# Reads of single words of k, q and w_in on ScalarE's queue in a gated-attention and MLP kernel

## The chip, the cores and the metric

One core of one Trainium2 chip runs the whole program. The metric is device time in microseconds (us), taken as the median of several runs. The engines are TensorE (PE; its weight loads are listed apart as PEld), VectorE (DVE), ScalarE (ACT), GpSimd (POOL) and SyncE (SP). In this kernel SP does no arithmetic; it issues DMAs.

## The reference

A gated linear attention over 4 batches, 8 heads, 768 tokens and head size 48 is followed by a two-layer MLP on 3072 tokens of width 384, with hidden width 2048. All data are float32.

```python
f = 1.0 / (1.0 + np.exp(-f_logit))                 # q, k, v, f_logit: (4, 8, 768, 48)
for t in range(S):
    state = f[:, :, t, :, None] * state + np.einsum('bhd,bhe->bhde', k[:, :, t], v[:, :, t])
    y[:, :, t] = np.einsum('bhd,bhde->bhe', q[:, :, t], state)
x = np.ascontiguousarray(y.transpose(0, 2, 1, 3)).reshape(B * S, H * D)     # (3072, 384)
h = x @ w_in                                       # w_in: (384, 2048)
g = np.maximum(0.01 * h, h)
out = g @ w_out                                    # w_out: (2048, 384)
```

## The kernel before

**Units.** The recurrence is worked in chunks of 128 tokens. The work is cut into 12 units. Units 0 to 3 are "paired": unit j takes the first two chunks (256 tokens, `2 * C`) of batch j, with two neighbouring tokens on each of 128 partitions, and its loads come in two halves of four heads each. Units 4 to 11 take one later chunk of two batches each.

**A unit's way.** `load` brings f, k, q and v from DRAM into the tiles `raw_fk` (f and k) and `raw_qv` (q and v). On ACT, `gate_e` and `gate_l` turn f into the log of the gate; PE sums it up over the chunk (`cs`); ACT makes decays of it (`dec`: the tiles `em`, `at` and `end`). `scale` multiplies k and q by decays, on DVE or POOL (tiles `kh` and `qh`); PE turns them (`tk`, `tq`), multiplies them to scores (`sc`), which DVE masks (`mk`), and mixes them with v (`mx`). `x_out` copies the result as `xT`. The MLP's first layer is `up` or `up_pair` (lines 510 and 521), ACT's leaky relu follows, `down` (line 532) is the second layer, `out_copy` and `store` bring the result out. `fill` puts matmuls of a constant tile on PE (line 135) that nothing reads.

**Weights.** `load_w_in` and `load_w_in_half` bring 512 or 256 columns of w_in, with row 128 k + p on partition p, into spare raw tiles; `cast_w` and `cast_w_in_half` make bfloat16 tiles of them on ACT, DVE or POOL. w_out follows in the same way.

**Order.** Nothing schedules the work: a long string, `order`, is read word by word, and each word calls a part of the kernel with its numbers (`Lk_0_1` loads the second half of unit 0's k; `dec_1_1` is the second decay of unit 1; `WI_2` loads the third 512 columns of w_in, the first weights that are loaded). So each engine's instructions stand in the string's order. All DMAs of the kernel are issued by SP's queue.

**Semaphores.** The framework under the kernel hands the DMAs eight semaphores in turn, named DMAHW0 to DMAHW7. Before a semaphore is used again, the issuing queue waits until the DMA that had it has landed; a reader of loaded data waits for the semaphore of its load.

Of the kernel before, what the change touches and what calls it, by code (L numbers as in the profile page):

```python
# [9 lines left out]
FP32 = mybir.dt.float32  # L10
# [5 lines left out]
def kernel(  # L16
# [10 lines left out]
    nc = tc.nc  # L27

    B, H, S, D = q.shape
    assert (B, H, S, D) == (4, 8, 768, 48)  # L30
    C = 128
# [3 lines left out]
    NK, NF = KD // 128, FF // 128  # L35
# [16 lines left out]
    const = ctx.enter_context(tc.tile_pool(name="const", bufs=1))  # L52
    psum = ctx.enter_context(tc.tile_pool(name="psum", bufs=1, space=bass.MemoryType.PSUM))
    ctx.enter_context(tc.manual_schedule())

    nc.scalar.preload_act_table_set("natural_log_exp_and_others")

    def tiles(n, shape, dtype, name):
        return [const.tile(shape, dtype, name=f"{name}{i}", tag=f"{name}{i}") for i in range(n)]
# [47 lines left out]
    def on(e):  # L107
        return nc.gpsimd if e else nc.vector
# [30 lines left out]
    w_in_b = tiles(NW, [128, NK, 512], BF16, "w_in")  # L139
    w_out_b = tiles(NW, [128, 4, KD], BF16, "w_out")  # L140

    def staging(i):
        t = (raw_fk, raw_qv)[i % 2][NB - 2 + i // 2]
        return t.rearrange("t x a h d -> t (x a h d)")
# [14 lines left out]
    def load(x):  # L159
        def go(j, a, e=0):  # L160
            queue = nc.scalar if e else nc.sync
            if paired(j):
                h = slice(0, H) if a == 2 else slice(4 * a, 4 * a + 4)
                queue.dma_start(out=by_pair(raw(j, x))[:, h].rearrange("t h s d -> t h (s d)"),  # L164
                                  in_=srcs[x][j, h, 0:2 * C, :].rearrange("h (t s) d -> t h (s d)", s=2))
            else:
                c, h = units[j]
                queue.dma_start(out=raw(j, x)[:, a],  # L168
                                  in_=srcs[x][2 * h + a, :, c * C:(c + 1) * C, :].rearrange("h t d -> t h d"))
        return go  # L170

    def load_w_in(i):
        nc.sync.dma_start(out=staging(i).rearrange("t (k n) -> t k n", k=NK),
                          in_=moe_w_in[:, 512 * i:512 * i + 512].rearrange("(k p) n -> p k n", p=128))

    def half_of(t, x):
        return t[:, :, 256 * x:256 * x + 256]
# [17 lines left out]
    def cast_w(to):  # L195
        def go(i, x, e):
            cols = slice(512 * x, 512 * x + 512)
            dst, src = to[i].rearrange("t k n -> t (k n)")[:, cols], staging(i)[:, cols]
            if e == 1:
                nc.scalar.copy(out=dst, in_=src)  # L200
            else:
                on(e).tensor_copy(out=dst, in_=src)
        return go
# [361 lines left out]
    def store(j, a):  # L565
# [7 lines left out]
        "sc": score, "mk": mask, "mx": mix, "ms": mix_state, "xt": x_out, "pt": state, "sf": state_add, "sb": state_end,  # L573
        "up": up, "pr": relu, "uw": up_pair, "pw": relu_pair, "dn": down, "ob": out_copy, "st": store,
        "Lf": load("f"), "Lk": load("k"), "Lq": load("q"), "Lv": load("v"),
        "We": load_w_in_half, "Ce": cast_w_in_half, "WI": load_w_in, "WO": load_w_out, "CI": cast_w(w_in_b), "CO": cast_w(w_out_b),
        "dh": down_half, "oh": out_half, "sh": store_half,
        "c0": constants, "zk": clear_pads, "pm": make_pair_mask, "zv": clear_v2, "zs": clear_state, "ut": make_ut,
        "F": fill,
# [5 lines left out]
    Lv_1_0 gl_1_0 Lv_0_1 dec_0_0 Lq_1_1 ck_0_1_0 Lk_1_0 zv_2_1 zs_0_1 pm_1 tq_0_1@3 Lf_2_0 Lv_1_1 v_0_0 v_0_1 v_1_0  # L585
    cs_1_0@4 Lq_1_0 Lf_2_1 ge_1_1 WI_2 cq_0_1_0 gl_1_1 We_0_0 sc_0_1@5.6 k_0_0_0 F_3@0 tk_0_0@7 q_0_0_0 We_1_1
    dec_1_0 Lq_2_1 k_1_0_1 mk_0_1_0 ck_0_0_1 tq_0_0@0 cs_1_1@2 cq_0_0_0 v_1_1 F_1@4 sc_0_0@1.3 F_4@0 pt_0_2@4.5
    mk_0_1_1 dec_1_1 k_1_1_0 tk_1_1@0 q_1_0_1 q_1_1_0 mk_0_0_0 mk_0_0_1 sf_0_0 F_8@6 tq_1_1@7 sb_0_0 mx_0_2@6.2
    ge_2_0 CI_2_1_2 cq_1_1_0 Ce_0_0_0_2 ck_1_1_0 Ce_0_0_1_2 Lk_2_0 tk_1_0@1 sc_1_1@3.4 pt_1_2@7.0 Lk_2_1 xt_0_0_1
    F_1@6 tq_1_0@6 gl_2_0 ge_2_1 ms_0 Lq_2_0 ck_1_0_1 We_1_0 mk_1_1_0 gl_2_1 sf_1_0 We_0_1 Lv_2_0 cs_2_1@3 cs_2_0@1  # L590
    cq_1_0_1 sb_1_0 Lv_2_1 xt_0_1_0 sc_1_0@7.6 WI_3 CI_2_0_1 Ce_1_1_0_2 Ce_1_1_1_2 CI_2_2_0 mk_1_1_1 F_1@2 up_0_4@2
# [89 lines left out]
```

## Time and profile before

| | |
|---|---|
| median of 3 runs | 176.87 us (176.82 to 177.32) |
| profiled execution | 177.9 us, its span 175.9 us |
| busy: PE, PEld, DVE, ACT, POOL | 167.3, 105.0, 83.5, 107.5, 64.8 us |
| granted PE clock | 0.999 of full speed |
| DRAM read, written | 25.17 MB, 4.72 MB |
| DMA packets on SP's queue | 110512, 34.61 MB |

The span runs from the first to the last instruction of the profiled execution; the profiled execution's own time is 2.0 us longer than its span. Busy times are sums over the span and overlap between engines. A line number (L164) is the kernel's line; `out<-in` names tiles; "SPq" is SP's queue, and for a DMA issue the time shown is that of the issue, not of the transfer. In brackets stands the idle time of the engine just before an instruction and what ended it. A row "DMA to landing" gives the time from the start of an issue until all of its data are there.

### The profile page before, as it was taken

The page shows a single profiled execution, that of the slowest core. Times are in us where ns is not written, and L with a number is a line of the kernel's source. Part 1 is how long each engine was busy: PE and PEld are TensorE (multiplying, and loading weights), DVE is VectorE, ACT ScalarE, POOL GpSimd, SP SyncE. Part 2 cuts the span into 40 slices and gives each one's busy share as a digit, 9 for nine tenths or more (in the row PEclk, how much of TensorE's full clock was granted, in tenths as well). Part 3 has the DMA queues.
Part 4 walks back from the last instruction along what each step waited for, and adds up shares of the span by engine and source line. Part 5 has one row for each costly group of instructions (what it writes and reads, how often), then busy time and mean ns, then how long its engine had stood idle before and what let it go on. Part 6 is the DMA issues. An engine that isn't in the chain of part 4 may idle for free.

```text
span 175.9 us, 5142 instructions
## 1 busy us (share of the span) xinstructions
PE 167.3 (95%) x2095; PEld 105.0 (60%) x2095; DVE 83.5 (47%) x169; ACT 107.5 (61%) x233; POOL 64.8 (37%) x149
## 2 busy tenths in 40 slices
PE   7788989999999999999999999999999999999993
PEld 2555678797666785744565754565734555645662
DVE  4488787555138407602465770838622308510010
ACT  4775497797753681499960489900599930477411
POOL 7558686353401972200266565001462222000000
PEclk9999999999999999999999999999999999999999
DMA  5999999999999889897999999999989994132004
GB/s 125 279 296 312 317 292 364 364 306 247 241 198 198 149 175 197 159 200 150 197 240 139 248 217 218 177 147 188 267 174 213 173 200 126 46 137 93 0 22 157
DMA packets 110535, 34.93 MB, mean 199 GB/s; under 512 B 102960, under 2 KB 109744, under 8 KB 110512
## 3 DMA queue, kind: packets, MB, share of 16 engines
q1 hardware_dynamic: 110512, 34.61, 85.2%
q8 instruction: 16, 0.26, 0.6%
q14 instruction: 7, 0.06, 0.1%
HBM read 25.17 MB, written 4.72 MB: 170 GB/s over the span
## 4 chain that ended last, share of the span: by engine, by line
PE 63%; DMA 13%; SPq 11%; issue 4%; POOL 3%; DVE 3%; ACT 1%; POOLq 0%; DVEq 0%
PE ps L532 24%; PE ps L521 19%; PE ps L510 9%; SPq L164 6%; DMA out_dram<-osb 6%; SPq L168 5%; DMA raw_fk<-in_moe_w_in_dram 4%; PE ps L393 3%; DMA kT<-kh 3%; PE ps L548 2%; PE ps L362 1%; DVE wm L376 1%; POOL kh L286 1%; PE ps L258 1%; PE ps L463 1%
## 5 line engine op out<-in xcount | busy, mean ns | idle before, releaser
L532 PE MATMUL ps<-w_out,gT 128*128 128x384 bf16 x368 | 65.8, 326 | 0.0
L532 PEld LDWEIGHTS <-gT 128*128 128x128 bf16 x368 | 34.3, 98 | 22.5
L521 PE MATMUL ps<-xT,w_in 128*128 128x512 bf16 x192 | 44.4, 379 | 0.5 <-DVE osb L543 0.5
L525 ACT ACTIVATE gT<-ps 128x512 bf16<-128x512 f32 x64 | 35.1, 631 | 6.1 <-PE ps L521 6.0
L521 PEld LDWEIGHTS <-w_in 128*128 128x128 bf16 x192 | 18.4, 98 | 21.4 <-issue 1.3
L376 DVE TENSOR_TENSOR wm<-ps,ut 128x512 bf16<-128x512 f32 x32 | 19.9, 683 | 15.8 <-PE ps L362 6.2
L291 POOL CAST vb<-raw_qv 128x384 bf16<-128x384 f32 (+1 forms) x16 | 10.6, 664 | 37.0 <-DMA raw_qv<-in_v_dram 36.8
L510 PE MATMUL ps<-xT,w_in 128*128 128x256 bf16 x192 | 23.3, 273 | 0.8 <-ACT xT L445 0.5
L543 DVE COPY osb<-ps 128x384 f32<-128x384 f32 x14 | 7.6, 554 | 31.9 <-PE ps L532 19.2
L516 ACT ACTIVATE gT<-ps 128x512 bf16<-128x512 f32 x32 | 17.6, 624 | 5.7 <-PE ps L510 5.5
L510 PEld LDWEIGHTS <-w_in 128*128 128x128 bf16 x192 | 18.2, 98 | 3.9 <-ACT w_in L200 0.5
L229 ACT ACTIVATE e<-raw_fk 128x384 f32<-128x384 f32 (+1 forms) x16 | 10.9, 689 | 15.1 <-DMA raw_fk<-in_f_logit_dram 14.9
L274 ACT ACTIVATE em<-ps 128x384 bf16<-128x384 f32 x24 | 12.2, 508 | 11.5 <-PE ps L261 10.0
L445 ACT CAST xT<-ps 128x384 bf16<-128x384 f32 x14 | 6.7, 502 | 16.8 <-PE ps L393 16.6
L483 POOL CAST sb<-sf 64x192 bf16<-64x192 f32 x40 | 13.7, 343 | 8.2 <-DVE sf L473 6.0
L480 POOL TENSOR_TENSOR sf<-sf,end 128x192 f32<-128x192 f32 x16 | 8.1, 505 | 19.0 <-DVE sf L475 18.6
L286 DVE TENSOR_TENSOR kh<-raw_fk,em 128x384 bf16<-128x384 f32 (+1 forms) x10 | 8.7, 866 | 13.5 <-DMA raw_fk<-in_k_dram 7.1
L475 DVE TENSOR_TENSOR sf<-sf,ps 64x192 f32<-64x192 f32 x32 | 11.2, 350 | 5.1 <-PE ps L463 2.2
L286 DVE TENSOR_TENSOR qh<-raw_qv,at 128x384 bf16<-128x384 f32 (+1 forms) x12 | 9.3, 789 | 8.3 <-ACT at L275 7.8
L275 ACT ACTIVATE at<-ps 128x384 bf16<-128x384 f32 x24 | 12.4, 515 | 0.0
L286 POOL TENSOR_TENSOR kh<-raw_fk,em 128x384 bf16<-128x384 f32 (+1 forms) x6 | 8.5, 1410 | 8.1 <-ACT em L274 3.6
L241 ACT ACTIVATE lf<-e 128x384 bf16<-128x384 f32 (+1 forms) x16 | 10.9, 684 | 0.3
(92 smaller groups left out, 182.5 us busy)
## 6 DMA issues: line engine op xcount, KB each, us to landing
out_dram<-osb SPq DMA_DIRECT2D x23, 192.0 KB, 3.2
raw_fk<-in_f_logit_dram SPq DMA_DIRECT2D x22, 192.0 KB, 4.0
raw_fk<-in_k_dram SPq DMA_DIRECT2D x22, 192.0 KB, 4.0
raw_qv<-in_q_dram SPq DMA_DIRECT2D x22, 192.0 KB, 4.0
raw_qv<-in_v_dram SPq DMA_DIRECT2D x22, 192.0 KB, 4.0
raw_fk<-in_moe_w_out_dram SPq DMA_DIRECT2D x2, 768.0 KB, 8.4
raw_qv<-in_moe_w_out_dram SPq DMA_DIRECT2D x2, 768.0 KB, 7.3
raw_fk<-in_moe_w_in_dram SPq DMA_DIRECT2D x1, 768.0 KB, 6.7
```

Source lines behind the costliest of these rows:

```text
L229: nc.scalar.activation(e[:, part], src[:, part], AF.Exp, scale=-1.0)
L274: nc.scalar.activation(ems[j % 2][:, a], t[:, 0:H * D], AF.Exp, scale=1.0)
L275: nc.scalar.activation(ats[j % 2][:, a], t[:, 0:H * D], AF.Exp, scale=-1.0)
L286: eng.tensor_mul(heads(j, to[j % NR], a)[:, :, :, 0:D], raw_heads(j, x, a), decays(j, by, a))
L376: nc.vector.tensor_mul(w, src.rearrange("t (p n) -> t p n", p=P2), ut[:, None, :].to_broadcast([128, P2, 128]))
L475: nc.vector.tensor_add(sf[rows], sf[rows], new)
L483: nc.gpsimd.tensor_copy(out=sb[rows, :, y * D:y * D + D], in_=sf[rows])
L510: nc.tensor.matmul(pm[:, i, :], w_in_of(ff, kk), xTs[j // 2 % 2][:, kk, j % 2].rearrange("t a s -> t (a s)"), start=(kk == 0), stop=(kk == ...
L516: nc.scalar.activation(dst, pm, AF.Prelu, alpha=0.01)
L521: nc.tensor.matmul(banks[bank], w_in_of(ff, kk), xTs[j // 2 % 2][:, kk].rearrange("t u a s -> t (u a s)"), start=(kk == 0), stop=(kk == NK ...
L525: nc.scalar.activation(g_blocks(j)[ff], banks[st[j].pop(("pm", ff))], AF.Prelu, alpha=0.01)
L532: nc.tensor.matmul(po, g_of(j, ff, a), w_out_b[quarter][:, ff % 4, :], start=(ff == 0), stop=(ff == NF - 1))
```

## The change

Three DMAs are added, all issued by ACT. None of the loads changes, and nothing reads the words.

- Two stand ahead of everything else on ACT, also ahead of its table load. They read batch 0 of k and of q: from each of 8 heads, the first element of every sixteenth of the first 256 tokens, 128 words of 4 bytes each, into 16 partitions of a small tile.
- One, `tw`, stands in `order` after `dec_1_1`. It reads element 1024 of every eighth row of w_in, 48 words, into 16 partitions. Column 1024 is the first of those that `WI_2` loads.

```diff
     ctx.enter_context(tc.manual_schedule())
+
+    first_words = const.tile([16, 2, H], FP32, tag="first_words")
+    for i, t in enumerate((k, q)):
+        nc.scalar.dma_start(out=first_words[:, i], in_=t[0, :, 0:2 * C:16, 0].rearrange("h t -> t h"))
 
     nc.scalar.preload_act_table_set("natural_log_exp_and_others")
...
+    row_words = const.tile([16, NK], FP32, tag="row_words")
+
+    def touch_w_in():
+        nc.scalar.dma_start(out=row_words, in_=moe_w_in[::8, 1024].rearrange("(k p) -> p k", p=16))
...
+        "We": load_w_in_half, "Ce": cast_w_in_half, "WI": load_w_in, "tw": touch_w_in, ...
...
-    mk_0_1_1 dec_1_1 k_1_1_0 tk_1_1@0 q_1_0_1 ...
+    mk_0_1_1 dec_1_1 tw k_1_1_0 tk_1_1@0 q_1_0_1 ...
```

The lines of the changed kernel lie 4 to 9 further down (`load` issues at L168 there, not L164), and tile numbers after an underscore move by 3. What moves on the engines is shown in rows of the two programs' orders. First ACT, from its first row on: `e` is written by `gate_e` from unit 0's f, `lf` by `gate_l`. Before:

```order
L676 UNCONDITIONAL_BRANCH
L56 ACT_TABLE_LOAD
L229 ACTIVATE e_76<-raw_fk_64 128x384
L241 ACTIVATE lf_78<-e_76 128x4x2x48
L229 ACTIVATE e_76<-raw_fk_64 128x384
```

And of the changed kernel, the same place on ACT:

```order
L685 UNCONDITIONAL_BRANCH
L58 DMA first_words<-in_k_dram 16x8x1
L58 DMA first_words<-in_q_dram 16x8x1
L60 ACT_TABLE_LOAD
L238 ACTIVATE e_79<-raw_fk_67 128x384
L250 ACTIVATE lf_81<-e_79 128x4x2x48
```

The two issues stand ahead of the table load and of the first gate; the rest of the row follows as before. The third one stands on ACT between the last decay of unit 1 (`em`, `at`, `end`) and the first gate of unit 2:

```order
L283 ACTIVATE em_91<-ps_160 128x384
L284 ACTIVATE at_93<-ps_160 128x384
L286 ACTIVATE end_95<-ps_160 128x2x2
L183 DMA row_words<-in_moe_w_in_dram 16x3x1
L238 ACTIVATE e_79<-raw_fk_69 128x384
```

Nothing else is inserted there. On SP the loads stand as before, but the new DMAs take three semaphores out of the turn, so that SP's waits are for other DMAs. These are SP's sixth to tenth DMAs with their waits (the halves of k and f of units 0 and 1, then q and v), before:

```order
L164 DMA raw_fk_64<-in_k_dram 128x4x96
L164 DMA raw_fk_65<-in_f_logit_dram 128x4x96
L164 DMA raw_fk_65<-in_k_dram 128x4x96
L164 DMA raw_qv_70<-in_q_dram 128x4x96 [waits DMAHW0_49]
L164 DMA raw_qv_70<-in_v_dram 128x4x96 [waits DMAHW1_49]
```

and in the changed kernel:

```order
L168 DMA raw_fk_67<-in_k_dram 128x4x96
L168 DMA raw_fk_68<-in_f_logit_dram 128x4x96 [waits DMAHW0_49]
L168 DMA raw_fk_68<-in_k_dram 128x4x96 [waits DMAHW1_49]
L168 DMA raw_qv_73<-in_q_dram 128x4x96 [waits DMAHW2_49]
L168 DMA raw_qv_73<-in_v_dram 128x4x96 [waits DMAHW3_49]
```

Semaphores 0 and 2 belong to the words of k and q here, 1 and 3 to the two halves of unit 0's f. So SP's first wait comes two DMAs earlier, at its seventh. Farther on, at the loads around the first weights, with their waits in the changed kernel:

```order
L168 DMA raw_qv_74<-in_q_dram 128x4x96 [waits DMAHW3_49]
L168 DMA raw_fk_69<-in_f_logit_dram 128x4x96 [waits DMAHW4_49]
L177 DMA raw_fk_72<-in_moe_w_in_dram 128x3x512 [waits DMAHW5_49]
L189 DMA raw_fk_71<-in_moe_w_in_dram 128x3x256 [waits DMAHW6_49]
L189 DMA raw_qv_77<-in_moe_w_in_dram 128x3x256 [waits DMAHW7_49]
L168 DMA raw_qv_75<-in_q_dram 128x4x96 [waits DMAHW0_49]
```

Semaphore 7 belongs to the words of w_in there: SP's twentieth DMA, the half of w_in into `raw_qv`, waits for them. From SP's thirteenth DMA to its nineteenth the wait is for the DMA seven places earlier in SP's queue, where it was eight before. On PE, DVE and POOL the instructions stand as they did.

More of the change, by code (lines that the diff above doesn't have):

```diff
@@ L575 @@
         "Lf": load("f"), "Lk": load("k"), "Lq": load("q"), "Lv": load("v"),
-        "We": load_w_in_half, "Ce": cast_w_in_half, "WI": load_w_in, "WO": load_w_out, "CI": cast_w(w_in_b), "CO": cast_w(w_out_b),
+        "We": load_w_in_half, "Ce": cast_w_in_half, "WI": load_w_in, "tw": touch_w_in, "WO": load_w_out, "CI": cast_w(w_in_b), "CO": cast_w(w_out_b),
         "dh": down_half, "oh": out_half, "sh": store_half,
@@ L587 @@
     dec_1_0 Lq_2_1 k_1_0_1 mk_0_1_0 ck_0_0_1 tq_0_0@0 cs_1_1@2 cq_0_0_0 v_1_1 F_1@4 sc_0_0@1.3 F_4@0 pt_0_2@4.5
-    mk_0_1_1 dec_1_1 k_1_1_0 tk_1_1@0 q_1_0_1 q_1_1_0 mk_0_0_0 mk_0_0_1 sf_0_0 F_8@6 tq_1_1@7 sb_0_0 mx_0_2@6.2
+    mk_0_1_1 dec_1_1 tw k_1_1_0 tk_1_1@0 q_1_0_1 q_1_1_0 mk_0_0_0 mk_0_0_1 sf_0_0 F_8@6 tq_1_1@7 sb_0_0 mx_0_2@6.2
     ge_2_0 CI_2_1_2 cq_1_1_0 Ce_0_0_0_2 ck_1_1_0 Ce_0_0_1_2 Lk_2_0 tk_1_0@1 sc_1_1@3.4 pt_1_2@7.0 Lk_2_1 xt_0_0_1
```

## The prediction

> **What bounds the kernel now.** I read the page first, for engine shares.
>
> ```profile
> span 175.9 us, 5142 instructions
> PE 167.3 (95%) x2095; PEld 105.0 (60%) x2095; DVE 83.5 (47%) x169; ACT 107.5 (61%) x233; POOL 64.8 (37%) x149
> q1 hardware_dynamic: 110512, 34.61, 85.2%
> ```
>
> TensorE (PE) is busy 95% of a span of 175.9 us; nothing else passes 61%. A change that adds no PE work can only pay where PE waits, so I next cut the span into stages, by what DMA delivers. Columns: stage, its length, busy time (and instructions) of PE, PEld, DVE, ACT, POOL, then granted clock, DMA share, GB/s.
>
> ```profile
> 0.00:2.50 2.50, 1.45 (x4) 0.58 (x5) 1.67 (x11) 1.28 (x1) 1.76 (x12) 1.00 0.17 38
> 2.50:3.50 1.00, 1.00 (x4) 0.30 (x2) 0.32 (x3) 0.00 (x0) 0.85 (x7) 1.00 1.08 296
> 3.50:5.50 2.00, 2.00 (x13) 0.98 (x12) 0.00 (x0) 1.93 (x5) 2.00 (x8) 1.00 0.93 208
> 5.50:8.00 2.50, 1.62 (x19) 1.10 (x18) 1.69 (x4) 1.65 (x6) 1.37 (x6) 1.00 1.13 304
> 8.00:14.50 6.50, 5.56 (x104) 3.65 (x108) 5.56 (x11) 4.74 (x14) 3.62 (x10) 1.00 1.10 293
> 14.50:16.00 1.50, 1.20 (x76) 0.92 (x79) 1.24 (x4) 0.67 (x2) 1.25 (x4) 1.00 0.87 273
> 16.00:19.30 3.30, 2.66 (x77) 1.92 (x70) 1.92 (x5) 2.21 (x6) 1.54 (x3) 1.00 1.05 359
> 24.00:80.00 56.00, 55.93 (x772) 39.86 (x772) 28.20 (x57) 38.71 (x84) 23.65 (x45) 1.00 0.98 233
> 80.00:172.00 92.00, 90.99 (x949) 52.12 (x948) 38.70 (x70) 53.24 (x116) 24.50 (x50) 1.00 0.78 162
> ```
>
> From 24 us PE is full: 55.93 of 56.00 us, then 90.99 of 92.00. There is no room there, and none of the change's instructions stand there. Before 24 us the DMA share is near or above 1 in every stage after 2.5 us, so the input stream sets the pace, and in one stage it delivers badly: 208 GB/s from 3.5 to 5.5 us, between stages of 296 and 304. At 296 GB/s the same bytes need 2.0 × 208 / 296 = 1.41 us, so **0.6 us** is missing. A second, weaker dip is 273 GB/s at 14.5 to 16.0.
>
> Third, the first loads one by one (start of the issue, in us, and time from issue to landing).
>
> ```profile
> L164 SPq DMA_DIRECT2D raw_fk<-in_f_logit_dram x2: 449/468/488, 0.7 to 1.2; - x2
> DMA to landing us min/median/max: 2.8/2.8/2.8
> L164 SPq DMA_DIRECT2D raw_fk<-in_k_dram x1: 499/499/499, 1.8 to 1.8; - x1
> DMA to landing us min/median/max: 4.2/4.2/4.2
> L164 SPq DMA_DIRECT2D raw_qv<-in_q_dram x1: 507/507/507, 2.3 to 2.3; - x1
> DMA to landing us min/median/max: 4.3/4.3/4.3
> L164 SPq DMA_DIRECT2D raw_fk<-in_f_logit_dram x1: 508/508/508, 2.9 to 2.9; - x1
> DMA to landing us min/median/max: 4.3/4.3/4.3
> L164 SPq DMA_DIRECT2D raw_fk<-in_k_dram x1: 507/507/507, 3.4 to 3.4; - x1
> DMA to landing us min/median/max: 4.4/4.4/4.4
> ```
>
> The two loads of f land at 0.7 + 2.8 = 3.5 and 1.2 + 2.8 = 4.0. The first of k lands at 1.8 + 4.2 = 6.0, 2.0 us behind. The next three, q, f of unit one and the second half of k, land at 6.6, 7.2 and 7.8: 0.6 apart. So the first load of k, and with it all behind it, is 2.0 − 0.6 = **1.4 us** late on the DMA engine that finishes last, 0.6 us on the mean of 16 (the dip). The second load of k has other rows of the same tensor and shows no gap. So the wait reads like one for the first access to a tensor, which is what the change aims at; that is my reading, no view names the cause.
>
> Fourth, what the late landings hold up.
>
> ```profile
> 0.73 1.28 ACT L56 ACT_TABLE_LOAD   x1 [0.73 <-PEq L665]
> 3.51 0.52 ACT L229 ACTIVATE e<-raw_fk 128x384 f32<-128x384 f32 x1 [1.50 <-DMA raw_fk<-in_f_logit_dram]
> 6.07 0.56 DVE L286 TENSOR_TENSOR kh<-raw_fk,em 128x384 bf16<-128x384 f32 x1 [3.25 <-DMA raw_fk<-in_k_dram]
> 7.24 0.52 ACT L229 ACTIVATE e<-raw_fk 128x384 f32<-128x384 f32 x1 [0.82 <-DMA raw_fk<-in_f_logit_dram]
> 12.52 6.74 DMA raw_fk<-in_moe_w_in_dram
> 16.48 0.91 POOL L286 TENSOR_TENSOR qh<-raw_qv,at 128x384 bf16<-128x384 f32 x1 [0.72 <-DMA raw_qv<-in_q_dram]
> 17.45 0.40 PE L319 MATMUL ps<-ident,qh 128*128 128x128 bf16 x4 [0.51 <-POOL qh L286]
> 19.37 0.28 PE L135 MATMUL ps<-filler 128*128 128x256 bf16 x1
> 19.95 2.31 PE L510 MATMUL ps<-xT,w_in 128*128 128x256 bf16 x18 [0.30 <-ACT w_in L200]
> ```
>
> ScalarE (ACT) waits 0.82 us for unit one's f at 7.24. The load of w_in at 12.52 is a link of 6.74 us in the chain that ended last, and PE's first matmul from w_in at 19.95, from which PE runs nearly full, waits 0.30 for its cast. Just ahead, a scaled q that its load held up to 16.48 (0.72) holds PE until 17.45 (0.51). All of these are landings of one stream: shift the stream by x and PE's full stretch starts about x earlier, up to some 0.8 (ACT's 0.82). Beyond, compute binds.
>
> **The change part by part.** *Issues of the first words.* Two DMA issues stand before the table load on ACT. No row shows a DMA issue on ACT; the nearest are SyncE's (SP's), 0.45 to 0.51 us here. The load of 1.28 us would then start at 0.73 + 1.0 and end at 3.0; the first gate starts at 3.51. Cost nothing, covered by the wait for f, with 0.5 to spare. From below there is no gain, since f's landing binds. From above: were each issue as long as SP's longest in these stages, 1.73 (next fence), the table would end at 0.73 + 3.5 + 1.28 = 5.5 and the gate be 2.0 late. I take nothing, by the row of the same kind in an unfilled queue.
>
> *Their packets.* 2 × 128 words are 16 packets for each of 16 engines. The page's q1 row prices a packet of 313 bytes on average (34.61 MB in 110512): 0.852 × 16 × 175.9 us / 110512 = 22 ns. So 0.35 us at most; 0 at least, since engines are idle for most of the first stage (share 0.17). I take 0.2.
>
> *What they give back.* If the words take the first access to k and q while the engines still start up on f, the 1.4 us (last engine) or 0.6 us (mean) go. Both waits count, since consumers wait for the last engine but the stream for all: I take the middle, 1.0. The floor is nothing, or below (rivals).
>
> [...]
>
> *SP's waits.* SP's loads share eight semaphores in turn with the words. Its seventh load now waits for the words of k, its ninth for those of q, and the twentieth DMA, half of w_in, for the words of w_in; behind these stands every later load.
>
> ```profile
> 3.98 1.38 SPq L164 DMA_DIRECT2D raw_fk<-in_f_logit_dram  x1
> 13.64 1.73 SPq L180 DMA_DIRECT2D raw_qv<-in_moe_w_in_dram  x1
> 15.42 1.01 SPq L164 DMA_DIRECT2D raw_qv<-in_q_dram  x1
> 13.62 0.52 ACT L229 ACTIVATE e<-raw_fk 128x384 f32<-128x384 f32 x1 [1.37 <-DMA raw_fk<-in_f_logit_dram]
> L164 SPq DMA_DIRECT2D raw_qv<-in_v_dram x1: 547/547/547, 7.9 to 7.9; - x1
> DMA to landing us min/median/max: 3.8/3.8/3.8
> ```
>
> The seventh was issued at 3.98 and its issue lasted until 5.36, where others last 0.5; I read that as a full queue. Words whose issue ends by 1.73 and that land 2.8 later, like the first loads, are there at 4.5; by then the queue has room, and an issue of 0.5 ends at 5.0, before 5.36. With 4.2 to landing, like k's, the words are there at 5.9 and SP is 1.0 late, while loads are under way that land until 7.8. Cost nothing; cover: 1.9 us of queued transfers. The half of w_in took from 13.64 to 15.37 for the same reason. The words of w_in are issued after unit one's decays, some time in ACT's idle 1.37 us before 13.62; at 12.3 plus the 3.8 to 4.4 us of loads in a full queue they land at 16.1 to 16.7, and with an issue of 0.5 SP is up to 1.8 later than 15.37. What lies in the queue then is the load issued at 12.52, landing at 19.26, and the half behind it. Cost nothing, cover 2.5 us; if it is gone, each us over it is a us of stream. Loads 13 to 19 wait for the seventh DMA before them, not the eighth. The nearest case, w_in at 12.5, then waits for a load of v that was issued at 7.9 and landed 3.8 later, at 11.7: 0.8 to spare. Cost nothing.
>
> *Words of w_in.* The dip at 14.5 looks like a repetition at the first access of w_in, but the loads around it say something else.
>
> ```profile
> L164 SPq DMA_DIRECT2D raw_qv<-in_q_dram x1: 632/632/632, 11.1 to 11.1; - x1
> DMA to landing us min/median/max: 5.3/5.3/5.3
> q8 instruction: 1, 0.02, 5.1%
> ```
>
> This load of q lands at 11.1 + 5.3 = 16.4, although it stands before w_in in the queue. In 13.5 to 15.0 one instruction packet (0.02 MB) held 5.1% of 16 engines × 1.5 us = 1.2 us of one engine. That explains most of the delay, and no word removes it. The 0.30 us of PE's wait for w_in is the most that is left: 0 to 0.3. I take 0, since PE is occupied till 19.65 anyhow by the row at 19.37.
>
> **The sum.** 1.0 given back, less 0.2 of packets: 0.8 us off, just what ACT's 0.82 allows. The profiled execution took 177.9 us, its span 175.9 and 2.0 around it; 177.9 becomes 177.1. The median of the runs shown is 176.87, 1.0 under the profiled one, so the forecast is 176.87 − 0.8 = **176.1 us**.
>
> **The rivals.** *First, slower: the words wait for themselves alone.* If what is waited for belongs to a row or a small region and to one DMA engine, each word pays its own wait, ahead of f, and k's load still pays its own. Price: the mean wait of 0.6 once more, plus packets of 0.2: 0.8, to 177.7; at most 0.6 + 0.35, to 177.8. It decides once f lands 0.5 later than 3.5 (then ACT's gates and decays move with it, since ACT is busy 1.93 of the 2.00 us from 3.5) while k still lands 2.0 behind f. Against it: the second half of k, other rows, had no gap. For it: nothing shows that a word read by one engine helps another engine.
>
> [...] No run here shows which engine moved what. [...]
>
> *Second, no change: the wait moves.* The first accesses hold the same engines from 1.8 us on, f lands late by what k is early, the stream is where it was. 0 plus 0.2 of packets: 176.9 to 177.1. For it: the DMA share stays 0.93 in the dip, so engines are held, not free for others. Against it: f's own first access shows no gap behind the 2.8 us.
>
> *Third, more: both dips close on the last engine.* 1.4 + 0.3 without cost: 1.7, 175.2. Against it: ACT's 0.82 and the instruction packet.
>
> **How the numbers follow.** Forecast 0.38, first rival 0.30, second 0.24, third 0.08. The runs shown spread by 0.3% (176.82 to 177.32), which is about what a measurement of this kernel can tell from no change: 0.53 us. Under 176.34 lie the third rival and nearly all of the forecast, less 0.04 where only half comes back: faster 0.42. Same: 0.24 + 0.04 = 0.28. Slower: 0.30. The range reaches from the third rival to the first's bound, 175.2 to 177.8. Cases of both signs hold the chance; the likeliest one's own range is 1.4 − 0 to 0.6 − 0.35 off: 175.5 to 176.6.
>
> **What would show it.** Right: k's first landing within 1 us of f's second, no stage under 280 GB/s between 3.5 and 5.5, the gate at 7.24 starting near 6.4, w_in's cast near 18.5. The first step is wrong if the gate at 3.51 starts over 0.3 later; the sum is wrong if w_in lands earlier and PE's full stretch doesn't. SP's waits are wrong if the load at 13.64 ends past 17 with lower GB/s behind it. The words of w_in are shown idle if q's load before them still takes over 5 us.

## The result and the profile after

The changed kernel takes **178.74 us** (median of 22 runs, 177.52 to 181.48), where the kernel before has 177.77 us in its 22 runs beside it (176.09 to 179.0). The ratio is 1.0104, with a 95% interval of 1.0074 to 1.0134. A second comparison (`e10_change_again` below) gives 1.0074 [1.0036, 1.0113]. Here and below a ratio leaves out the runs counted as slow, those over 1.5% above the fastest run of the same kernel, while a median leaves out none. So the change makes the kernel slower: by 0.7 to 1.0%, some 1.3 to 1.8 us, in the ratios, and by 1.0 and 1.3 us in the medians. The forecast was 176.1 us and faster; its range ended at 177.8.

The profiled execution of the changed kernel took 180.12 us, its span is 178.2 us at a granted clock of 0.981. These are its stages, in the columns of the prediction's first table (length, busy time of PE, PEld, DVE, ACT and POOL, granted clock, DMA share, GB/s).

```profile
2.50:3.50 1.00, 1.00 (x4) 0.30 (x2) 0.32 (x3) 0.57 (x1) 0.85 (x7) 1.00 1.14 286
3.50:5.50 2.00, 1.89 (x14) 0.99 (x13) 0.00 (x0) 1.77 (x4) 2.00 (x8) 1.00 0.91 200
5.50:8.00 2.50, 1.70 (x19) 1.04 (x18) 1.80 (x4) 1.61 (x6) 1.33 (x6) 1.00 1.23 280
8.00:14.50 6.50, 4.98 (x73) 3.30 (x74) 4.46 (x9) 4.47 (x13) 2.65 (x7) 0.74 1.28 263
16.00:19.30 3.30, 2.75 (x120) 2.08 (x118) 2.36 (x6) 2.28 (x6) 2.22 (x6) 1.00 1.03 357
```

The dip that the change was to fill is still there, 200 GB/s from 3.5 to 5.5 us (208 before). What is new comes behind it, at 5.5 to 14.5 us, when the first words have long landed: 280 and 263 GB/s where there were 304 and 293. The DMA engines are not idle for that. Their share has risen from 1.13 and 1.10 to 1.23 and 1.28, so they are busier and move less. Counted in bytes, 2.5 × 24 + 6.5 × 30 = 255 KB are missing by 14.5 us, which at 293 GB/s is **0.9 us** of stream.

The DMA view of 8 to 14 us says what the engines do with their time. The row has queue, packets, MB, and the packets' time as a share of 16 engines × 6 us. Before:

```profile
q1 hardware_dynamic: 4699, 1.75, 108.8%
```

and in the changed kernel:

```profile
q1 hardware_dynamic: 4204, 1.57, 126.9%
```

A packet took 1.088 × 96 us / 4699 = 22.2 ns, and now takes 1.269 × 96 / 4204 = 29.0 ns. Nearly all of these packets are pieces of 384 bytes (4558 of the 4699, and 4076 of the 4204; the others are of 4 bytes): 4 heads × 2 tokens × 48 numbers are 1536 bytes in a partition, and arrive as four such pieces. Same pieces, same source, 30% more time each. Their times overlap (the share is over 100%), so the packets that start in these 6 us fall by less, from 4699 to 4204, a factor of 1.12.

The pieces of the changed kernel aren't slow from the start. From 5.0 to 5.5 us its queue has 405 packets at a share of 110.3%, which is 1.103 × 8 us / 405 = 21.8 ns each, and from 5.5 to 6.0 us it delivers 317 GB/s (319 before). From 7.0 to 8.0 us it delivers 260 (289 before). The pieces and their places are of the same kind in both stretches; why the cost sets in at about 6 us is open.

What the late stream holds up is seen in the timeline of ACT, then of PE, in the changed kernel (start, duration, instruction, and in brackets the idle time before it and what ended it).

```profile
3.67 0.52 ACT L238 ACTIVATE e<-raw_fk 128x384 f32<-128x384 f32 x1 [0.59 <-DMA raw_fk<-in_f_logit_dram]
7.39 0.52 ACT L238 ACTIVATE e<-raw_fk 128x384 f32<-128x384 f32 x1 [0.86 <-DMA raw_fk<-in_f_logit_dram]
14.90 0.52 ACT L238 ACTIVATE e<-raw_fk 128x384 f32<-128x384 f32 x1 [1.50 <-DMA raw_fk<-in_f_logit_dram]
20.58 0.62 ACT L209 CAST w_in<-raw_fk 128x512 bf16<-128x512 f32 x1 [0.80 <-DMA raw_fk<-in_moe_w_in_dram]
11.09 0.61 PE L328 MATMUL ps<-ident,qh 128*128 128x128 bf16 x4 [1.00 <-DVE qh L295]
21.25 2.17 PE L519 MATMUL ps<-xT,w_in 128*128 128x256 bf16 x9 [0.67 <-ACT w_in L209]
```

Two rows of the kernel before, besides those that the prediction shows:

```profile
19.28 0.62 ACT L200 CAST w_in<-raw_fk 128x512 bf16<-128x512 f32 x1 [0.51 <-DMA raw_fk<-in_moe_w_in_dram]
10.35 0.40 PE L319 MATMUL ps<-ident,qh 128*128 128x128 bf16 x4 [0.42 <-DVE qh L286]
```

ACT's gate at 13.62 starts at 14.90, w_in's cast at 20.58 for 19.28, PE's first matmul from w_in at 21.25 for 19.95, and PE waits 1.00 us for a q at 11.09 where it waited 0.42. The two stretches 8.0 to 14.5 and 19.3 to 24.0 have granted clocks of 0.74 and 0.70, both 1.00 before. The clock is not what slows the stream: in `e10_change_again` the clock is 1.00 in both and the stream is as slow (below).

### The profile page after: what moved, and what is told of

Its sections match the earlier page's. It is cut to its first block, busy times and chain, and to the rows that moved or that the text cites. A ratio compares the mean times of both kernels' runs of the same rounds, so it can differ in the third digit from the quotient of the medians.

```text
span 178.2 us, 5145 instructions
## 1 busy us (share of the span) xinstructions
PE 168.9 (95%) x2095; PEld 106.3 (60%) x2095; DVE 83.4 (47%) x169; ACT 107.4 (60%) x233; POOL 64.5 (36%) x149
## 4 chain that ended last, share of the span: by engine, by line
PE 81%; DMA 8%; SPq 7%; DVE 1%; ACT 1%; issue 1%; DVEq 0%
PE ps L541 33%; PE ps L530 22%; PE ps L519 13%; SPq L168 7%; PE ps L402 5%; DMA raw_fk<-in_moe_w_in_dram 4%; DMA out_dram<-osb 4%; PE ps L371 2%; PE ps L557 1%; PE ps L267 1%; DVE wm L385 1%; PE ps L472 1%; PE ps L364 1%; PE ps L270 1%; PE ps L467 1%
## 5 line engine op out<-in xcount | busy, mean ns | idle before, releaser
L541 PEld LDWEIGHTS <-gT 128*128 128x128 bf16 x368 | 34.2, 98 | 22.5
L530 PEld LDWEIGHTS <-w_in 128*128 128x128 bf16 x192 | 18.4, 98 | 21.5 <-issue 1.2
L519 PE MATMUL ps<-xT,w_in 128*128 128x256 bf16 x192 | 24.8, 284 | 1.1 <-ACT w_in L209 0.7
L519 PEld LDWEIGHTS <-w_in 128*128 128x128 bf16 x192 | 19.0, 102 | 5.0 <-ACT w_in L209 0.9
L454 ACT CAST xT<-ps 128x384 bf16<-128x384 f32 x14 | 6.7, 503 | 18.0 <-PE ps L402 17.8
L295 DVE TENSOR_TENSOR kh<-raw_fk,em 128x384 bf16<-128x384 f32 (+1 forms) x10 | 7.8, 782 | 15.1 <-ACT em L283 9.0
```

The costliest lines, as they stand in the source:

```text
L295: eng.tensor_mul(heads(j, to[j % NR], a)[:, :, :, 0:D], raw_heads(j, x, a), decays(j, by, a))
L519: nc.tensor.matmul(pm[:, i, :], w_in_of(ff, kk), xTs[j // 2 % 2][:, kk, j % 2].rearrange("t a s -> t (a s)"), start=(kk == 0), stop=(kk == ...
L530: nc.tensor.matmul(banks[bank], w_in_of(ff, kk), xTs[j // 2 % 2][:, kk].rearrange("t u a s -> t (u a s)"), start=(kk == 0), stop=(kk == NK ...
L541: nc.tensor.matmul(po, g_of(j, ff, a), w_out_b[quarter][:, ff % 4, :], start=(ff == 0), stop=(ff == NF - 1))
```

## Experiments

The diff changes the place of things in a way that the prediction doesn't mention. `first_words` is the first tile allocated in the kernel, and tiles are laid one behind another in each partition. A tile of 2 × 8 numbers of 4 bytes takes 64 bytes of every partition, though only 16 partitions use it. In the built programs the first raw tile lies at byte 16512 of its partition before (129 × 128) and at 16576 in the changed kernel. All raw tiles are multiples of 128 bytes long, so every piece of 384 bytes of units 0 to 3 began on a multiple of 128 before, and begins 64 bytes behind one now. This is theory A, **moved tiles**: a piece of 384 bytes then touches four blocks of 128 bytes instead of three, and takes longer. Its rival is the **words' traffic**: the small reads, their issues or SP's waits for them take the time. All ratios are against the kernel before on the same chip, with 10 to 12 runs of the kernel and 23 to 35 of before.

### The tiles without the words

`e1_tiles_only` keeps both small tiles and drops all three DMAs.

```diff
     first_words = const.tile([16, 2, H], FP32, tag="first_words")
-    for i, t in enumerate((k, q)):
-        nc.scalar.dma_start(out=first_words[:, i], in_=...)
...
     row_words = const.tile([16, NK], FP32, tag="row_words")
-    def touch_w_in(): ...
...
-    mk_0_1_1 dec_1_1 tw k_1_1_0 ...
+    mk_0_1_1 dec_1_1 k_1_1_0 ...
```

> The two small tiles are allocated where the change has them, but none of the three DMAs is issued, so every other tile lies 64 bytes further on in its partition, and nothing else differs from before. Theory A (the place of the tiles): the 384-byte pieces of the first loads now begin 64 bytes off, the stream from 5.5 to 14.5 us falls to 263 to 280 GB/s as in the changed kernel (before: 304 and 293), and the time is 0.6 to 1.0% over before, nearly all of the change's 1.0%. Theory B (the words hold the engines): no difference, within 0.3% of before. Theory C (SP's wait for the words of w_in): no difference either.

Measured: 177.99 us against 176.73, ratio 1.007 [1.0027, 1.0113]. Its stage and its packets from 8 us on:

```profile
8.00:14.50 6.50, 5.13 (x86) 3.41 (x86) 4.81 (x11) 4.12 (x13) 3.00 (x9) 1.00 1.29 263
q1 hardware_dynamic: 4211, 1.57, 128.1%
```

263 GB/s, 1.281 × 96 / 4211 = 29.2 ns a packet. An unused tile alone makes the slow stream and a loss that can't be told from the change's. (`row_words` is kept too, but lies behind all large tiles and moves none of them.)

### The words without the move

`e2_words_at_end` has all three DMAs, but `first_words` is allocated behind all other large tiles. `e3_first_words_at_end` is the same without the words of w_in. `e4_row_words` has the words of w_in alone (`row_words` stands behind the large tiles in the change already).

```diff
-    first_words = const.tile([16, 2, H], FP32, tag="first_words")
-    for i, t in enumerate((k, q)):
-        nc.scalar.dma_start(...)
-
-    nc.scalar.preload_act_table_set("natural_log_exp_and_others")
...
     w_out_b = tiles(NW, [128, 4, KD], BF16, "w_out")
+    first_words = const.tile([16, 2, H], FP32, tag="first_words")
+    for i, t in enumerate((k, q)):
+        nc.scalar.dma_start(...)
+
+    nc.scalar.preload_act_table_set("natural_log_exp_and_others")
```

> All three DMAs as in the change, but the tile for the first words is allocated behind all others, so every tile that the kernel before has lies where it lay before. Theory A (the place of the tiles): 5.5 to 14.5 us is back at 290 to 304 GB/s, and the time is within 0.4% of before. Theory B (the words hold the engines ahead of f): still 0.6 to 1.0% over before, with the first f landing at 3.6 and the second at 4.4 as in the changed kernel. Theory C (SP's wait for the words of w_in): still 0.6 to 1.0% over before, with SP's twentieth DMA issued near 16.9.

> Only the words of k and q, none of w_in, and the tile behind all others. Theory A (the place of the tiles): within 0.4% of before. Theory B: 0.4 to 1.0% over before. Theory C: within 0.3% of before, SP's twentieth DMA issued near 13.6 again. In the trace it shows what the first words do to k: by my forecast the first load of k lands at 5.0 or earlier, by the trace of the changed kernel near 5.9.

> Only the words of w_in, no words of k and q, and no tile moved. Theory A (the place of the tiles) and theory B (the first words): within 0.3% of before. Theory C (SP's wait for the words of w_in): 0.5 to 1.0% over before, with SP's twentieth DMA issued 2 us or more after the nineteenth and the loads behind it late at their readers.

Measured: 176.65, 177.01 and 176.56 us against 176.73; ratios 0.9992 [0.9951, 1.0032], 0.9999 [0.996, 1.0038] and 0.999 [0.9951, 1.0029]. All three deliver as before from 8 us on. For `e2_words_at_end`, the stages at the dip and behind it, and the packets:

```profile
3.50:5.50 2.00, 2.00 (x8) 1.06 (x7) 0.00 (x0) 1.90 (x4) 2.00 (x8) 1.00 1.04 257
8.00:14.50 6.50, 5.87 (x143) 4.05 (x144) 5.83 (x12) 4.43 (x14) 4.01 (x10) 1.00 1.10 292
q1 hardware_dynamic: 4636, 1.73, 109.1%
```

So the words, their issues on ACT and SP's waits for them cost nothing that these runs can tell, and they give nothing back that the times show. The 257 GB/s in the dip look like the forecast's gain, but `e1_tiles_only`, which reads no word, has 263 there.

### Other moves

`e5_shift_32` and `e6_shift_128` are the kernel before with an unused tile of 32 or 128 bytes ahead of all others. `e7_words_padded` is the change with its tile stretched from 64 to 128 bytes. `e8_rest_shifted` leaves the raw tiles where they were and moves all tiles behind them by 64 bytes.

```diff
# e5, e6
+    shift = const.tile([128, 8], FP32, tag="shift")      # e6: [128, 32]
     nc.scalar.preload_act_table_set("natural_log_exp_and_others")
# e7
-    first_words = const.tile([16, 2, H], FP32, tag="first_words")
+    first_words = const.tile([16, 2, 2 * H], FP32, tag="first_words")
...
-        nc.scalar.dma_start(out=first_words[:, i], ...
+        nc.scalar.dma_start(out=first_words[:, i, 0:H], ...
# e8
     raw_qv = tiles(NB, [128, 2, 2, H, D], FP32, "raw_qv")
+    shift = const.tile([128, 16], FP32, tag="shift")
     es = tiles(2, [128, 2, H * D], FP32, "e")
```

> The kernel before with an unused tile of 32 bytes ahead of all others, so all its tiles lie 32 bytes further on; no words are read. Theory A (a piece of a load costs more when it does not start on a multiple of 128 bytes in its partition): the 384-byte pieces of units 0 to 3 touch four blocks of 128 bytes in place of three, as with 64 bytes, so 8.0 to 14.5 us runs near 263 GB/s. From unit 4 on, pieces of 192 bytes touch 2.5 blocks on average, where they touch 2 both before and with 64 bytes: the later loads now slow down too, and the time is 0.7% or more over before. Rival A64 (only the offset of 64, not alignment as such): 290 GB/s and the time of before, within 0.3%.

> The kernel before with an unused tile of 128 bytes ahead of all others; no words are read. Theory A with blocks of 128 bytes: every piece is cut as before, 8.0 to 14.5 us runs near 293 GB/s, the time is within 0.3% of before. Theory A with blocks of 256 bytes: the 384-byte pieces cost as before, but the weights' pieces of 1024 and 2048 bytes start on a block now, so 16.0 to 19.3 us runs above the 359 GB/s of before and the time is 0 to 0.3% lower. Rival (any move of the tiles away from where they were tuned costs): 0.5 to 1.0% over before.

> The change whole, all three DMAs at their places and the small tile ahead of all others, but that tile takes 128 bytes in place of 64. Theory A: the time of before within 0.4%, 8.0 to 14.5 us near 293 GB/s; the whole cost of the change is gone by 64 unused bytes. Theory B (the words themselves cost): still 0.6 to 1.0% over before.

> The kernel before with an unused tile of 64 bytes behind the raw tiles, so that the tiles that the loads write stay where they were and all others (gates, decays, scaled k and q, turned k and q, states, weights in bfloat16, the output tiles) lie 64 bytes further on. Theory A, told of the writes of the loads: within 0.3% of before, 8.0 to 14.5 us near 293 GB/s. Rival A2 (the engines' own reads and writes of the shifted tiles): 0.6 to 1.0% over before, with engine instructions longer than before.

Measured, with the time of a packet worked out as above from each kernel's row of the DMA view at 8 to 14 us:

| kernel | raw tiles begin at, mod 128 | GB/s at 8.0 to 14.5 us | ns a packet | us (before) | ratio, 95% interval |
|---|---|---|---|---|---|
| before | 0 | 293 | 22.2 | | |
| the change | 64 | 263 | 29.0 | 178.74 (177.77) | 1.0104 [1.0074, 1.0134] |
| `e1_tiles_only` | 64 | 263 | 29.2 | 177.99 (176.73) | 1.007 [1.0027, 1.0113] |
| `e5_shift_32` | 32 | 262 | 29.1 | 178.72 (176.63) | 1.011 [1.0075, 1.0146] |
| `e6_shift_128` | 0 | 277 | 22.7 | 177.25 (176.63) | 1.0037 [1.0, 1.0075] |
| `e7_words_padded` | 0 | 291 | 22.5 | 177.48 (176.63) | 0.9991 [0.9946, 1.0036] |
| `e8_rest_shifted` | 0 | 286 | 22.7 | 177.02 (176.63) | 1.0027 [0.9993, 1.0061] |

These are the rows of `e5_shift_32`, `e6_shift_128`, `e7_words_padded` and `e8_rest_shifted`, in this order:

```profile
q1 hardware_dynamic: 4220, 1.57, 127.8%
q1 hardware_dynamic: 4542, 1.69, 107.6%
q1 hardware_dynamic: 4629, 1.72, 108.4%
q1 hardware_dynamic: 4608, 1.72, 109.0%
```

In this stretch the packet's time knows only the remainder: 29 ns at 32 or 64, 22 to 23 ns at 0, whether words are read or not. `e7_words_padded` is the closest pair with the change: the same DMAs, the same order, 64 bytes more of unused tile, and the stream and the packets are those of before. On the time it says less: its ratio is 0.9991, but the median of its twelve runs is 0.5% above before's. For the time the pair of `e1_tiles_only`, with the loss and no word, and `e2_words_at_end`, with all the words and no loss in ratio or median, says more. `e8_rest_shifted` shows that a move of the other tiles alone doesn't slow the stream. The 277 of `e6_shift_128` isn't a slower packet: its DMA share there is 1.05, lower than any other kernel's, so its engines waited for something in that one profiled execution, which took 179.19 us. The interval of its ratio begins at 1.0, so a small cost of any move, the rival in its expectation, isn't excluded by the times; for the stream the packet's time excludes it.

A shift of 32 does more than one of 64. Loads of the later units, 4 to 11, come in pieces of 192 bytes, two neighbours of which fill three blocks of 128. Moved by 64 bytes, each piece still touches two blocks; moved by 32, every second one touches three. The DMA view of 80 to 172 us, when only later units are loaded beside the weights and the stores, first for the kernel before, then for `e1_tiles_only`, then for `e5_shift_32`:

```profile
q1 hardware_dynamic: 57142, 14.77, 77.6%
```

```profile
q1 hardware_dynamic: 57428, 15.07, 78.4%
```

```profile
q1 hardware_dynamic: 59034, 15.05, 87.2%
```

0.784 × 16 × 92 us / 57428 = 20.1 ns a packet, and 0.872 × 1472 / 59034 = 21.7; 20.0 before. These are means over packets of all sizes; the packets of 192 bytes alone take 15.7 ns before, 15.6 in `e1_tiles_only` and 18.2 in `e5_shift_32`. There the 32 costs engine time too, and the 64 doesn't, as the count of blocks has it. What is delivered doesn't fall: 165 GB/s in both, 162 before.

In the packets' time the trace has a factor of 29.0 / 22.2 = 1.31, in their number one of 1.12. The blocks themselves are the author's theory; no view shows one. If their count is what costs, blocks of 64 bytes are ruled out, since a move by 64 would change nothing; with blocks of 128 the factor is 4/3. Whether the block is 128 or 256 these runs don't tell. The sign that `e6_shift_128` was to give for 256, more than 359 GB/s from 16.0 to 19.3 us, isn't there (321, and 309 in `e7_words_padded`, whose tiles begin on a multiple of 256 as well), but the weights' pieces hardly know a move at all: from 14 to 24 us the medians over the kernels are 46 to 47 ns for 1024 bytes and 84 to 88 ns for 2048. And no count of blocks has the moved pieces at 22 ns before 6 us.

### What the dip is

The forecast took the late first load of k for a first access to that tensor. `e9_k_q_from_f` is the kernel before with unit 0's loads of k and q reading the rows of f.

```diff
-    in_=srcs[x][j, h, 0:2 * C, :]...
+    in_=srcs["f" if j == 0 and x in "kq" else x][j, h, 0:2 * C, :]...
```

> The kernel before, with no word read ahead and no tile moved, but unit zero's loads of k and q read the rows of f (the outputs are then computed from other data; sizes, order and addresses on the chip are those of before). If the gap of 1.3 to 2.0 us between f's second landing and k's first, seen in every kernel so far, is a first access to the tensor k, it shrinks to about 0.6 (the distance of the loads after it), the stretch from 3.5 to 5.5 us delivers 290 GB/s or more instead of 208 to 260, and the time falls by 0.6 to 1.0 us. If the gap belongs to the start of the stream (the fourth and later loads stand behind one another in the queue, whatever they read), it stays at 1.3 to 2.0 with 205 to 265 GB/s, and the time stays within 0.5 us of before.

Measured: 177.43 us against 177.12, ratio 1.001 [0.997, 1.0049]. The profiled execution is one of two (the other is of the kernel before) that took 428 us, with TensorE busy for 418.50 of 425 us, over twice as long as before (167.3 of 175.9), at a granted clock of 1.00; only its DMAs up to 5.5 us are read here, which were issued at the times of the others. The loads of f, then of what is k in other kernels (here two loads of f in one group, the second is that in k's place):

```profile
3.50:5.50 2.00, 2.00 (x4) 0.43 (x3) 0.00 (x0) 1.83 (x4) 2.00 (x8) 1.00 1.01 262
L164 SPq DMA_DIRECT2D raw_fk<-in_f_logit_dram x2: 483/491/499, 1.3 to 1.8; - x2
DMA to landing us min/median/max: 3.0/3.6/4.2
```

The load in k's place lands at 1.8 + 4.2 = 6.0 us, as k did (1.8 + 4.2), though it reads f, and rows of it that the first load has read already. In this profile the gap belongs to the third load of the stream, not to the tensor. The trace has the landing on each of 16 engines: here the median of them is at 4.6 and the last at 6.0; before, 4.9 and 6.0. So one engine falls behind, or a few. Later loads keep a spread of 1.2 to 1.6 us between the first engine and the last, and their last landings are 0.6 apart again. Why an engine falls behind there is open. The mean over engines did improve, 262 GB/s for 208, but `e1_tiles_only` with k's own rows has 263, and the time didn't move.

### The change again

> The change once more, on the chip of the run beside it, to see which of its marks repeat. The theory of moved tiles (the 64 bytes of the first words' tile stand ahead of all others, so the 384-byte pieces of the loads of units zero to three begin at another remainder of 128) expects 0.7 to 1.4 percent over before, 260 to 266 GB/s from 8.0 to 14.5 us against 286 to 297 in before, at the same DMA share or a higher one, and k's first landing between 5.3 and 5.9. The rival (words in the way of the stream) has nothing that would lower the rate there after 8 us, when the first words have landed long before, and expects 286 to 297.

Measured: 178.39 us against 177.12, ratio 1.0074 [1.0036, 1.0113]. Its profiled execution took 177.63 us, span 175.7 us, and runs at full clock:

```profile
8.00:14.50 6.50, 4.93 (x85) 3.33 (x85) 4.32 (x10) 4.31 (x13) 2.83 (x8) 1.00 1.28 262
19.30:24.00 4.70, 4.60 (x124) 3.52 (x123) 4.13 (x10) 2.46 (x6) 3.57 (x8) 1.00 1.16 293
q1 hardware_dynamic: 4205, 1.57, 127.2%
```

262 GB/s and 1.272 × 96 / 4205 = 29.0 ns a packet again. k's first load lands at 5.72, inside the bounds expected. PE starts with w_in at 20.62, 0.67 later than before, with the clock at 1.00. That its span is no longer than before's profiled 175.9 is the scatter of single executions: its twelve runs lie between 176.88 and 180.07 us, those of before, but for one, between 175.87 and 178.28.

## Why the prediction was wrong, step by step

**The starting point**: too low by 0.9. The forecast starts from 176.87 us, the median of three runs; over 22 runs the median before is 177.77. In medians, the 2.6 us between forecast and result are about 0.9 from here, 0.8 that didn't come, and 1.0 that the change costs.

**What bounds the kernel**: right. The input stream sets the pace until about 20 us, and slower packets in it (29.2 ns for 22.2 in `e1_tiles_only`) make the kernel slower (ratio 1.007). But 0.9 us of stream stand beside 1.3 to 1.8 us in the ratios and 1.0 to 1.3 in the medians; whether there is a difference to explain, and what makes it up, isn't settled. The granted clock is a candidate: it is below 0.995 in 11 of the 22 runs of the change, whose medians with and without are 179.3 and 178.34. That PE's longer waits bring the lower clock is a guess of the author's that no run shows.

**The issues of the first words**: right. The issues take 0.45 and 0.54 us, the table load runs from 1.79 to 3.07, and the first gate still waits 0.59 us for f.

```profile
0.74 0.45 ACTq L58 DMA_DIRECT2D first_words<-in_k_dram  x1
1.22 0.54 ACTq L58 DMA_DIRECT2D first_words<-in_q_dram  x1
1.79 1.28 ACT L60 ACT_TABLE_LOAD   x1 [1.79 <-issue]
```

**Their packets**: 0.2 was taken. The first gate starts 0.16 later (3.67 for 3.51), 0.08 in `e10_change_again`; `e2_words_at_end` and `e3_first_words_at_end` have it at 3.42 and 3.44. The price was too high: from 1.0 to 3.5 us ACT's queue has 274 packets at a share of 6.1%, 0.061 × 40 us / 274 = 8.9 ns each for 22, so 16 of them make 0.14 us. Nothing that the times can tell.

**What they give back**: wrong, the step of the sum that failed first. It was 1.0 us, and with the words read and no tile moved the times show none of it (ratios of 0.9992 and 0.9999). In the changed kernel f's second load and k's first, one group here, take 3.1 and 4.1 us to land:

```profile
L168 SPq DMA_DIRECT2D raw_fk<-in_f_logit_dram x1: 489/489/489, 1.2 to 1.2; - x1
L168 SPq DMA_DIRECT2D raw_fk<-in_k_dram x1: 500/500/500, 1.8 to 1.8; - x1
DMA to landing us min/median/max: 3.1/3.6/4.1
```

That is 4.4 and 5.9 on the clock. In the trace's finer numbers k lands 1.50 us behind f in the change and 1.91 before, 1.29 in `e1_tiles_only` without words, and 1.57 and 1.10 with words in `e2_words_at_end` and `e3_first_words_at_end`. Over all profiles it is 1.10 to 1.67 in the five kernels that read the first words and 1.29 to 2.09 in the seven that don't; of the 0.3 between their means, half is f's own later landing. So a small gain isn't excluded, and 1.0 is. In `e3_first_words_at_end`, which has the earliest, k lands at 5.25, between the 5.0 of the forecast and the 5.9 of the change. The reading of the gap as a first access, on which the 1.0 stood, fell with `e9_k_q_from_f`. That the second half of k shows no gap, which the prediction took as a sign of it, fits as well with a gap that any third load has.

**SP's waits**: the mechanism was right, its delay larger, its price still nothing. SP's half of w_in, second row here, waits for the words of w_in until 16.89.

```profile
14.06 0.49 SPq L189 DMA_DIRECT2D raw_fk<-in_moe_w_in_dram  x1
16.89 0.37 SPq L189 DMA_DIRECT2D raw_qv<-in_moe_w_in_dram  x1
17.30 0.49 SPq L168 DMA_DIRECT2D raw_qv<-in_q_dram  x1
```

From 14.55 to 16.89 SP stands idle, 2.3 us, and the q behind goes out at 17.30 for 15.42 before, 1.9 late where 1.8 was the estimate. The stage from 16.0 to 19.3 still delivers 357 GB/s (359), and `e2_words_at_end` and `e4_row_words`, where SP stands idle there for 2.1 and 1.0 us, lose nothing: the cover of 2.5 us held.

**The words of w_in**: 0 taken, 0 measured (`e4_row_words`). The q's load ahead of them takes 4.6 us to land in the change's profile, and 5.5 in that of `e10_change_again` (issued at 11.55, there at 17.09), so the words don't reliably take its delay away. Over the profiles it is 3.8 to 5.5 us in the five kernels that read words of w_in and 4.8 to 6.3 in six that don't (5.3 before), so a shorter delay isn't excluded; the times show nothing of it. The weaker dip at 14.5 to 16.0, 273 GB/s before, is at 336 to 354 in `e2_words_at_end`, `e3_first_words_at_end`, `e4_row_words` and `e7_words_padded`, and the second of these reads no word of w_in, so the dip isn't w_in's first access either. That the instruction packet is the cause, as the prediction argued, was not tried.

**The missing term**: the sum has no line for the tile's place. The text says that none of the loads changes, and of their instructions that is true; the address they write to wasn't looked at. The order of the instructions doesn't show addresses, and the profile of before can't show a move. But the diff's first line is an allocation ahead of all others in the same pool, and its size is 64 bytes; that could have been a rival on the slow side: 293 GB/s less the price of a fourth block.

**The rivals**: the first, slower, forecast 177.7 and came closer than the forecast, by luck: words that pay their own wait were nowhere seen, and f's first load lands 0.15 later, not 0.5. The second, no change, has the time that the words alone give (`e2_words_at_end` to `e4_row_words`). Its reason, that the wait for the first access moves from k to f, isn't shown: `e9_k_q_from_f` has the gap where no row of k has been accessed yet. Of the signs named in advance, k within 1 us of f's second, 280 GB/s in the dip, the gate at 7.24 near 6.4 (it is at 7.39) and the cast near 18.5 (20.58) all failed.

None of the kernels run here is faster than the kernel before by more than its interval.

## What to carry to other kernels

Read a new tile as a change of every address behind it: here the first raw tile went from byte 16512 to 16576. Allocate small or odd-sized tiles last, or pad them to a multiple of 128 bytes, above all ahead of tiles that take many short DMA pieces: from 8.0 to 14.5 us these two had 292 and 291 GB/s (`e2_words_at_end`, `e7_words_padded`) where the change had 263. A share of DMA time that rises while GB/s fall, here from 1.10 to 1.28 with 293 to 263, is the sign to look for. And before a gap is named after what is loaded, load something else in its place: the same late landing, 6.0 us, was there for other rows.

## What the runs showed of the hardware

- From 8 to 14 us a DMA piece of 384 bytes took 22 ns where its destination begins on a multiple of 128 bytes and 29 ns at 32 or 64 bytes behind one; from 8.0 to 14.5 us the stream fell from 293 to 263 GB/s with the engines busier (1.28 for 1.10). Up to about 6 us the moved pieces took 22 ns as well. Pieces of 192 bytes were untouched by 64 (15.6 ns in the later stage, 15.7 before) and slowed by 32 (18.2).
- The granted clock fell below 0.995 in 30 of 58 runs of the kernels with moved raw tiles (the change, `e10_change_again`, `e1_tiles_only`, `e5_shift_32`), in 13 of 72 of `e2_words_at_end` to `e4_row_words` and `e6_shift_128` to `e8_rest_shifted`, and in 17 of the 93 of the kernel before beside the experiments. In the change's profile it is half for two stretches of 3.4 us:

```profile
11.00:14.40 3.40, 3.31 (x39) 2.04 (x41) 3.08 (x7) 1.51 (x6) 2.55 (x7) 0.50 1.27 260
21.20:24.60 3.40, 3.35 (x16) 2.32 (x17) 2.74 (x7) 0.50 (x2) 2.81 (x7) 0.50 1.03 258
```

In the 3.4 us ahead of each, at full clock, PE was busy for 1.71 us (7.6 to 11.0) and for 2.19 us (17.8 to 21.2); before, in the same places and with no half clock behind them, for 2.39 and 2.98. What sets the clock these runs don't tell.

- Two executions of 45 in the last comparison, one of them of the kernel before, took 428 us at a granted clock of 1.00, with PE busy for 418.50 of 425 us in the profile of `e9_k_q_from_f`, where before's profile has 167.3 of 175.9. What slows them is not in the trace.
